# An elementwise sum moved from VectorE to an accumulating DMA, with its consumers a quarter-step later

## The chip, the cores and the metric

The kernel runs on one core of a Trainium2 chip. The metric is device time of one execution in microseconds, where less is better: the median of three runs before the change is 296.59 us (296.36 to 297.35).

## What is computed

Attention over 4 batches, 8 heads, 768 positions and head size 64, in which each query sees the first 4 positions and a window of its own last 128, is followed by a two-layer block on the 3072 x 512 result. The part that the change touches is the function between the two matrix products, a quotient of polynomials taken for every one of 3072 x 2048 elements:

```
h = x @ w_in                      # 3072 x 512 by 512 x 2048
P = a[0] + a[1]*h + a[2]*h*h + a[3]*h*h*h
Q = 1 + |b[0]|*|h| + |b[1]|*h*h
g = P / (Q + 1e-6)
out = g @ w_out                   # 3072 x 2048 by 2048 x 512
```

## The kernel before, in words

The 3072 rows are cut into NSTEP = 12 steps of 256 rows. For each step there is an attention part (scores, exponentials, a mask, the product with v, a normalization, a transpose) and a part of the block: the first GEMM (`project_in`, L419), the function, and the second GEMM (`project_out`, L500). h of a step is one tile `hb` of 128 partitions x 4096 columns in bf16, and all intermediate tiles of the function (`sq`, `den`, `num`, `g`) have this shape. One such tile is 1 MB.

The order on every engine is written out by hand in one loop over t, a "slot". Four slots make a step: t = 4p + j. In slot t, TensorE computes a quarter of the first GEMM of step p, some scores and attention products of steps ahead, and a quarter of the second GEMM of an older step; ScalarE copies h out of PSUM, takes exponentials, and takes the reciprocal of Q as exp(-ln Q) in two passes; VectorE does the polynomials. With c = p - 1, the function runs through these places:

- j = 0: `magnitude` (L449) and `square` (L443) of half B of step c, `recip_den` (ScalarE, L486) of half B of step c - 1, `denominator` (L454) of half A
- j = 1: `log_den` (ScalarE, L480) of half A, `denominator` of half B, and `gate(c - 1)` (L492), g = num * (1/Q)
- j = 2: `log_den` of half B, `even(c)` (L460), which writes num = a2*h² + a0, and `odd(c)` (L465), which turns sq into a3*h² + a1
- j = 3: `odd_h(c)` (L470), sq = sq*h, then `numerator(c)` (L474), num = num + sq, and the first half of the next square on ScalarE (L441)

Between these VectorE also normalizes the attention results as they come (L381, L384), multiplies masks (L348) and spreads transposed k (L293). Each engine takes its instructions in the written order, so an instruction that waits holds up all that stand behind it. `num` has a single buffer: even(c) can't write before gate(c - 1) has read.

`project_out` of step m starts in slot 4m + 10, the slot after gate(m), as `back = t - 10` says, and takes four slots, two for each 128 rows. `store` copies a finished result from PSUM (ScalarE, L505) and sends it off (L507).

DMAs are issued from two places. SP's queue carries the stores and the transposes of x (L407), k (L284) and q (L265). GpSimd's queue (POOL) carries the loads that cast from float32 to bf16: w_in, w_out, k (L131), q (L118) and v (L151). In slot 4p + 2, `feed` puts two loads of k and two of q on it, six steps ahead of c; in slot 4p, `load_v` puts eight loads of v on it. A load waits until its buffer is free: k and q for the transposes that read the buffer before, v for the attention products of an older step.

The numbers of the loop that the change touches:

```
for t in range(NSLOT + 14):
    back = t - 10
```

Of the kernel before, what the change touches and what calls it, by code (L numbers as in the profile page):

```python
# [13 lines left out]
ALU = mybir.AluOpType  # L14
# [3 lines left out]
def kernel(  # L18
# [13 lines left out]
    nc = tc.nc  # L32
# [130 lines left out]
    def load_w_out(part):  # L163
        for c in range(part * NFFC // 2, (part + 1) * NFFC // 2):
            nc.gpsimd.dma_start(out=w_out_sb[c], in_=moe_w_out[c * P:(c + 1) * P, :])
# [20 lines left out]
    for e in range(2):  # L186
        lo = e * 64
        nc.gpsimd.affine_select(
            out=edge[lo:lo + 64, 0, :], in_=edge[lo:lo + 64, 0, :], pattern=[[1, 64]],
            compare_op=ALU.is_ge, fill=0.0, base=0, channel_multiplier=-1)  # L190
        nc.gpsimd.affine_select(
            out=edge[lo:lo + 64, 1, :], in_=edge[lo:lo + 64, 1, :], pattern=[[-1, 64]],
# [12 lines left out]
    for h in range(H):  # L205
        nc.gpsimd.dma_start(out=v_sink[16 * h:16 * h + NS, :, h, 0:D],
                            in_=v[:, h, 0:NS, :].rearrange("b s d -> s b d"))
# [78 lines left out]
    def spread_k(s):  # L286

        b, g = divmod(s, GPB)
        src = kT_flat.pop(s)
        kT = kT_fix[s % 2]  # L290
        for e in range(2):
            lo, hi = e * 64, (e + 1) * 64
            nc.vector.tensor_copy(out=kT[lo:hi, :, lo:hi],  # L293
                                  in_=src[lo:hi].rearrange("p i (j c) -> p (i j) c", c=64))
        if g == 0:
            nc.vector.tensor_copy(
                out=k_sink[b % 2].rearrange("p (i c) -> p i c", c=160)[:, :, 0:32].rearrange(
                    "p i (e s) -> p i e s", e=2)[:, :, :, 0:NS],
                in_=kT.rearrange("p (i n) (e s) -> p i n e s", n=NHF, e=2)[:, :, 0, :, 0:NS])
# [112 lines left out]
    hb, sq, den, num, g_of, lnq, ps_h, ps_out = {}, {}, {}, {}, {}, {}, {}, {}  # L412

    def project_in(m, j):
        ps = ps_hp.tile([P, GC, TS], FP32, tag="ps_h", name="ps_h")
        for n in range(GC):
            fc = j * GC + n
            for c in range(NDMC):
                nc.tensor.matmul(ps[:, n, :], lhsT=w_in_sb[c][:, fc * P:(fc + 1) * P],  # L419
                                 rhs=xblk[m][:, c, :], start=(c == 0), stop=(c == NDMC - 1))  # L420
        ps_h[m, j] = ps
# [7 lines left out]
    def cols(w, part=None):  # L429

        if part is None:
            return slice(0, MW)
        k_, n = part
        return slice(k_ * MW // n, (k_ + 1) * MW // n)

    def square(m, part, eng):
        if m not in sq:
            sq[m] = m_sb.tile([P, MW], BF16, tag="sq", name="sq")
        c = cols(MW, part)
        if eng == "act":  # L440
            nc.scalar.activation(out=sq[m][:, c], in_=hb[m][:, c], func=AF.Square)  # L441
        else:
            nc.vector.tensor_tensor(out=sq[m][:, c], in0=hb[m][:, c], in1=hb[m][:, c], op=ALU.mult)  # L443

    def magnitude(m, part=None):
        if m not in den:
            den[m] = m_sb.tile([P, MW], BF16, tag="den", name="den")
        c = cols(MW, part)
        nc.vector.tensor_scalar(out=den[m][:, c].bitcast(U32), in0=hb[m][:, c].bitcast(U32),  # L449
                                scalar1=0x7FFF7FFF, scalar2=None, op0=ALU.bitwise_and)  # L450

    def denominator(m, part=None):
        c = cols(MW, part)
        nc.vector.tensor_tensor(out=den[m][:, c], in0=den[m][:, c], in1=sq[m][:, c], op=ALU.add)  # L454
# [16 lines left out]

    def numerator(m, part=None):
        c = cols(MW, part)
        nc.vector.tensor_tensor(out=num[m][:, c], in0=num[m][:, c], in1=sq[m][:, c], op=ALU.add)  # L474

    def log_den(m, part):
        c = cols(MW, part)
        t_ = m_sb.tile([P, HW], FP32, tag="lnq", name="lnq")
        lnq[m, part] = t_[:, 0:c.stop - c.start]
        nc.scalar.activation(out=lnq[m, part], in_=den[m][:, c], func=AF.Ln, scale=qsc,  # L480
                             bias=one_eps)

    def recip_den(m, part):
        c = cols(MW, part)
        with nc.allow_low_precision(reason="exp(-ln(q)) reciprocal, tol 2e-2"):
            nc.scalar.activation(out=den[m][:, c], in_=lnq[m, part], func=AF.Exp, scale=-1.0)  # L486
# [16 lines left out]
    def store(m, tt):  # L503
        o_t = o_sb.tile([P, DM], FP32, tag="o_t", name="o_t")
        nc.scalar.activation(out=o_t, in_=ps_out.pop((m, tt)), func=AF.Copy)  # L505
        row0 = m * TS + tt * P
        nc.sync.dma_start(out=out[row0:row0 + P, :], in_=o_t)  # L507
# [6 lines left out]
    NSLOT = 4 * NSTEP  # L514
# [3 lines left out]
    def feed(s):  # L518
        if s < NSTEP:
            load_k(s)  # L520
            for n in (2 * s + 1, 2 * s + 2):
                if n < NQT:
                    load_q(n)

    def turn_qk(s):
        if s < NSTEP:
            turn_k(s)
            for n in (2 * s + 1, 2 * s + 2):
                if n < NQT:
                    turn_q(n)  # L530
# [13 lines left out]
    def do_mask(n):  # L544
        s, i = divmod(n, NPB)
        if s < NSTEP and i % 2 == 1:
            mask(s, i // 2)
# [6 lines left out]
    def do_norm(n):  # L554
        s, i = divmod(n, NPB)
        if s < NSTEP:
            normalize(s, i)
            if i % 2 == 1:
                turn_x(s, i // 2)
# [48 lines left out]
    turn_at = {0: 2, 2: 3, 4: 4, 6: 5}  # L608
    stored = []
    prev_s, prev_a = (), ()  # L610
    for t in range(NSLOT + 14):
        p, j = divmod(t, 4)
        in_m = p < NSTEP
        ns = ahead_s.get(t, (t + 8,))
        na = ahead_a.get(t, (t + 6,))
        c = p - 1
        in_c = 0 <= c < NSTEP
        in_g = 0 <= c - 1 < NSTEP
        back = t - 10
        in_o = 0 <= back < NSLOT  # L620
        if stored:
            store(*stored.pop(0))
        for n in prev_a:
            do_norm(n)
        for n in prev_s:
            do_mask(n)
        if in_m:
            project_in(p, j)
        late = t > 7 and (t + 10) % NPB == 0
        if t == 0:  # L630
            turn_qk(1)
            spread_k(1)
        s = spread_at.get(t, (t + 10) // NPB if late else NSTEP)
        if s < NSTEP:
            spread_k(s)
        s = turn_at.get(t, (t + 14) // NPB if late else NSTEP)
        if s < NSTEP:
            turn_qk(s)
            if s != 3:
                feed(s + 2)  # L640
        if t in (4, 5):
            load_w_out(t - 4)
        if t == 5:
            feed(5)

        if j == 0:
            if in_c:
                magnitude(c, B_)
                square(c, B_, "dve")
            if in_g:  # L650
                recip_den(c - 1, B_)
            if in_c:
                denominator(c, A_)
        if j == 1:
            if in_c:
                log_den(c, A_)
                denominator(c, B_)
            if in_g:
                gate(c - 1)
        if j == 2:  # L660
            if in_c:
                log_den(c, B_)
                even(c)
        if j == 3:
            if in_c:
                recip_den(c, A_)
        if in_m:
            copy_in(p, j)
        if t < 4:
            for n in ns:  # L670
                do_sinks(n)
                do_scores(n)
                do_mask(n)
            for n in na:
                do_attend(n)
                if n != na[-1]:
                    do_norm(n)
        else:
            for n in ns:
                do_sinks(n)  # L680
                do_scores(n)
        if j == 2 and in_m:
            magnitude(p, A_)
        if in_o:
            m, gq = divmod(back, 4)
            tt, part = divmod(gq, 2)
            project_out(m, tt, part * NFFC // 2, (part + 1) * NFFC // 2)
            if part == 1:
                stored.append((m, tt))
        if t >= 4:  # L690
            for n in na:
                do_attend(n)
                if n != na[-1]:
                    do_norm(n)
        if j == 2 and in_c:
            odd(c)
        if j == 3:
            if in_c:
                odd_h(c)
                numerator(c)  # L700
            if in_m:
                square(p, A_, "act")
        prev_s = ns if t >= 4 else ()
        prev_a = na[-1:]
        if t >= 3 and (t == 3 or t > 4 and t % NPB == 0):
            s = 3 if t == 3 else (t + 8) // NPB
            if 3 <= s < NSTEP:
                load_v(s)
# [33 lines left out]
```

The softmax here doesn't subtract the row's maximum and nothing guards it: scores larger than these inputs give would overflow.

## Time and profile before

| | |
|---|---|
| median of three runs | 296.59 us |
| profiled execution, its own time | 298.49 us |
| its span | 296.8 us |
| mean granted TensorE clock | 0.96 |
| `numerator` L474 | 12 instructions, 27.5 us, 2292 ns each |
| `gate` L492 | 12 instructions, 27.4 us, 2284 ns each |
| loads of v, k, q from POOL | 4.4, 5.4 and 5.9 us from issue to landing (medians) |
| stores, 256 KB each | 2.4 us to landing (median) |
| chain that ended last, by engine | DVE 56%, PE 16%, DMA 8%, ACT 7%, issue 6%, SPq 5% |

In the profile, PE is TensorE, DVE VectorE, ACT ScalarE and POOL GpSimd; SPq is SP's queue. "L474" is line 474 of the kernel. A timeline line has the start and the length in microseconds, the engine, the line, the operation, what it writes and reads, and in brackets the idle time before it with what ended it. In a table of stretches each engine's busy time is given in microseconds, with the number of instructions. The ends of matmuls are modelled, so PE's busy time is an upper bound on its work.

### The profile page before, as it was taken

The numbers are of one execution on the slowest core, as the hardware profiler recorded it, in microseconds if no ns is written. First come the engines' busy times: TensorE is split into PE (matmuls) and PEld (weight loads), VectorE is DVE, ScalarE is ACT, GpSimd is POOL, SyncE is SP. The second block draws the span as 40 slices with busy tenths as digits, with TensorE's granted clock in tenths as the row PEclk, the third lists the DMA queues.
The fourth block names the chain that finished last, engine by engine and source line by source line (L and its number), as shares of the span: only waits on it lengthen the run. The fifth ranks groups of instructions, "written<-read, shape, count | busy, mean of one in ns | idle before, by whom it ended". The sixth has DMA issues, their size and how long they took to land.

```text
span 296.8 us, 4876 instructions
## 1 busy us (share of the span) xinstructions
PE 235.5 (79%) x1856; PEld 167.4 (56%) x1876; DVE 239.3 (81%) x320; ACT 214.2 (72%) x201; POOL 116.1 (39%) x178
## 2 busy tenths in 40 slices
PE   0516866658609899999989899998999999997864
PEld 0414555546507777767767677676677767652321
DVE  6606623736794999999999999999999999999930
ACT  2104261684735998989979899898998989897810
POOL 8938668879091046181651793380000000000000
PEclk9999997996957999999999999999999999997999
DMA  8999999999999199398995999292110121100111
GB/s 160 127 171 80 157 127 158 142 171 201 143 114 47 29 129 128 80 136 108 116 103 105 147 107 121 27 140 63 55 41 17 53 55 53 38 35 35 71 38 72
DMA packets 116632, 28.94 MB, mean 98 GB/s; under 512 B 110464, under 2 KB 112512, under 8 KB 116608
## 3 DMA queue, kind: packets, MB, share of 16 engines
q0 software_dynamic: 72752, 12.74, 64.1%
q1 hardware_dynamic: 43856, 15.88, 26.6%
q8 instruction: 15, 0.25, 0.4%
q14 instruction: 9, 0.07, 0.1%
HBM read 27.30 MB, written 6.29 MB: 113 GB/s over the span
## 4 chain that ended last, share of the span: by engine, by line
DVE 56%; PE 16%; DMA 8%; ACT 7%; issue 6%; SPq 5%; POOL 1%; DVEq 0%; ACTq 0%; POOLq 0%
DVE sq L470 8%; DVE num L474 8%; PE ps_h L419 7%; DVE g L492 6%; DVE den L454 6%; DVE x_n L384 5%; DVE num L460 4%; DVE den L449 4%; DVE e L348 4%; PE ps_out L500 4%; DVE sq L443 3%; PE ps_o L371 3%; DMA b_bc<-in_moe_b_dram 3%; DVE sq L465 2%; ACT hb L426 2%
## 5 line engine op out<-in xcount | busy, mean ns | idle before, releaser
L419 PE MATMUL ps_h<-xblk,w_in_sb 128*128 128x256 bf16 x768 | 98.5, 284 | 8.3 <-DMA xblk<-x_n 7.5
L500 PE MATMUL ps_out<-w_out_sb,g 128*128 128x512 bf16 x364 | 87.8, 385 | 7.6 <-ACT o_t L505 4.0
L419 PEld LDWEIGHTS <-w_in_sb 128*128 128x128 bf16 x768 | 76.4, 102 | 20.5 <-DMA xblk<-x_n 7.8
L151 POOL DMA_DIRECT2D v_bd<-in_v_dram x88 | 57.3, 670 | 28.7 <-PE ps_o L371 12.2
L426 ACT ACTIVATE hb<-ps_h 128x1024 bf16<-128x1024 f32 x48 | 49.1, 1022 | 26.2 <-PE ps_h L419 26.2
L500 PEld LDWEIGHTS <-g 128*128 128x128 bf16 x384 | 37.3, 99 | 45.6 <-issue 7.0
L480 ACT ACTIVATE lnq<-den,one_eps,qsc 128x2048 f32<-128x2048 bf16 x24 | 50.4, 2098 | 10.9 <-DVE den L454 10.9
L486 ACT ACTIVATE den<-lnq 128x2048 bf16<-128x2048 f32 x24 | 46.2, 1924 | 0.0
L341 ACT ACTIVATE e<-ps_s 128x768 bf16<-128x768 f32 x48 | 38.9, 816 | 2.8 <-PE ps_s L331 2.8
L131 POOL DMA_DIRECT2D k_bf<-in_k_dram x22 | 20.3, 937 | 46.9 <-DMA kT_flat<-k_bf 46.6
L371 PE MATMUL ps_o<-v_bd,e 128*128 128x130 bf16 x352 | 31.4, 228 | 9.1 <-DVE x_n L384 4.2
L331 PE MATMUL ps_s<-qT,kT 128*128 128x192 bf16 x192 | 25.7, 260 | 14.9 <-ACT e L341 14.6
L371 PEld LDWEIGHTS <-e 128*128 128x128 bf16 x352 | 26.1, 102 | 19.4 <-DVE x_n L384 4.9
L454 DVE TENSOR_TENSOR den<-den,sq 128x2048 bf16<-128x2048 bf16 x24 | 29.0, 1215 | 0.0
L331 PEld LDWEIGHTS <-kT 128*128 128x128 bf16 x192 | 18.4, 104 | 17.7 <-issue 16.2
L474 DVE TENSOR_TENSOR num<-num,sq 128x4096 bf16<-128x4096 bf16 x12 | 27.5, 2292 | 0.4
L492 DVE TENSOR_TENSOR g<-num,den 128x4096 bf16<-128x4096 bf16 x12 | 27.4, 2284 | 0.1
L470 DVE TENSOR_TENSOR sq<-sq,hb 128x4096 bf16<-128x4096 bf16 x12 | 27.4, 2284 | 0.1
L384 DVE SCALAR_TENSOR_TENSOR x_n<-ps_o,csc,rec 128x256 bf16<-128x256 f32 x48 | 23.2, 484 | 1.7
L381 DVE RECIPROCAL rec<-ps_o 128x4 f32<-128x4 f32 x48 | 8.5, 177 | 18.7 <-PE ps_o L371 18.5
L348 DVE TENSOR_TENSOR e<-e,edge 128x1024 bf16<-128x1024 bf16 x24 | 16.4, 683 | 8.3 <-ACT e L341 8.3
L441 ACT ACTIVATE sq<-hb 128x2048 bf16<-128x2048 bf16 x12 | 22.9, 1910 | 0.0
(67 smaller groups left out, 205.8 us busy)
## 6 DMA issues: line engine op xcount, KB each, us to landing
out_dram<-o_t SPq DMA_DIRECT2D x24, 256.0 KB, 2.4
k_bf<-in_k_dram POOLq DMA_DIRECT2D x22, 128.0 KB, 5.4
v_bd<-in_v_dram POOLq DMA_DIRECT2D x88, 32.0 KB, 4.4
q_bf<-in_q_dram POOLq DMA_DIRECT2D x21, 128.0 KB, 5.9
w_in_sb<-in_moe_w_in_dram POOLq DMA_DIRECT2D x8, 256.0 KB, 7.6
w_out_sb<-in_moe_w_out_dram POOLq DMA_DIRECT2D x16, 128.0 KB, 5.0
stage_q<-in_q_dram SPq DMA_DIRECT2D x3, 256.0 KB, 5.2
xblk<-x_n SPq DMA_TRANSPOSE x40, 3.5
```

The costliest lines, as they stand in the source:

```text
L151: nc.gpsimd.dma_start(out=t_[lo:hi, i, :, e, 0:D], in_=src)
L331: nc.tensor.matmul(ps[:, n // 2, (n % 2) * 192:(n % 2) * 192 + 192], lhsT=kT_fix[s % 2][:, i * NHF + n, :], rhs=qT_fix[b % 2][:, i, c:c + ...
L371: nc.tensor.matmul(ps_o[:, n, :], lhsT=l_, rhs=r_.rearrange("p e c -> p (e c)"), start=(m == 0), stop=(m == len(terms) - 1))
L419: nc.tensor.matmul(ps[:, n, :], lhsT=w_in_sb[c][:, fc * P:(fc + 1) * P], rhs=xblk[m][:, c, :], start=(c == 0), stop=(c == NDMC - 1))
L426: nc.scalar.activation(out=hb[m][:, j * GW:(j + 1) * GW], in_=ps_h.pop((m, j)).rearrange("p n c -> p (n c)"), func=AF.Copy)
L454: nc.vector.tensor_tensor(out=den[m][:, c], in0=den[m][:, c], in1=sq[m][:, c], op=ALU.add)
L470: nc.vector.tensor_tensor(out=sq[m][:, c], in0=sq[m][:, c], in1=hb[m][:, c], op=ALU.mult)
L474: nc.vector.tensor_tensor(out=num[m][:, c], in0=num[m][:, c], in1=sq[m][:, c], op=ALU.add)
L480: nc.scalar.activation(out=lnq[m, part], in_=den[m][:, c], func=AF.Ln, scale=qsc, bias=one_eps)
L486: nc.scalar.activation(out=den[m][:, c], in_=lnq[m, part], func=AF.Exp, scale=-1.0)
L492: nc.vector.tensor_tensor(out=g_of[m][:, c], in0=num[m][:, c], in1=den[m][:, c], op=ALU.mult)
L500: nc.tensor.matmul(ps_out[m, tt], lhsT=g_of[m][:, co:co + P], rhs=w_out_sb[fc], start=(fc == 0), stop=(fc == NFFC - 1))
```

## The change

`numerator` no longer runs on VectorE. It becomes a DMA from GpSimd's queue that reads `sq` and adds it into `num`, both in SBUF. The row of 4096 bf16 elements is cut at 4096 bytes, so that the compiled DMA is 128 x 2 x 2048 elements. There are twelve of them, one for each step, and in GpSimd's written order the one of step c stands behind the k and q loads of slot 4p + 2 and before the eight v loads of slot 4(p + 1).

`gate(c - 1)` moves from slot j = 1 to slot j = 2, where it stands before even(c) and behind that slot's normalization, mask and spread. `project_out` and with it the stores move one slot later, and the loop has one slot more.

```
     def numerator(m, part=None):
         c = cols(MW, part)
-        nc.vector.tensor_tensor(out=num[m][:, c], in0=num[m][:, c], in1=sq[m][:, c], op=ALU.add)
+        nc.gpsimd.dma_start(out=num[m][:, c], in_=sq[m][:, c], accum_op=ALU.add, max_dma_last_dim=4096)
...
-    for t in range(NSLOT + 14):
+    for t in range(NSLOT + 15):
...
-        back = t - 10
+        back = t - 11
...
             if in_c:
                 log_den(c, A_)
                 denominator(c, B_)
+        if j == 2:
             if in_g:
                 gate(c - 1)
-        if j == 2:
             if in_c:
                 log_den(c, B_)
                 even(c)
```

More of the change, by code (lines that the diff above doesn't have):

```diff
@@ L473, in numerator @@
         c = cols(MW, part)
-        nc.vector.tensor_tensor(out=num[m][:, c], in0=num[m][:, c], in1=sq[m][:, c], op=ALU.add)
+        nc.gpsimd.dma_start(out=num[m][:, c], in_=sq[m][:, c], accum_op=ALU.add, max_dma_last_dim=4096)
     def log_den(m, part):
@@ L610 @@
     prev_s, prev_a = (), ()
-    for t in range(NSLOT + 14):
+    for t in range(NSLOT + 15):
         p, j = divmod(t, 4)
@@ L618 @@
         in_g = 0 <= c - 1 < NSTEP
-        back = t - 10
+        back = t - 11
         in_o = 0 <= back < NSLOT
@@ L657 @@
                 denominator(c, B_)
+        if j == 2:
             if in_g:
                 gate(c - 1)
-        if j == 2:
             if in_c:
```

## The prediction

> **What bounds the kernel now.** I read first the busy times of the engines.
>
> ```profile
> PE 235.5 (79%) x1856; PEld 167.4 (56%) x1876; DVE 239.3 (81%) x320; ACT 214.2 (72%) x201; POOL 116.1 (39%) x178
> ```
>
> No engine stands out over the whole span, so I went to stretches: one step in mid-run, and the last two between numerators.
>
> ```profile
> core 0: us, PE busy (x) PEld busy (x) DVE busy (x) ACT busy (x) POOL busy (x), PEclk, DMA share, GB/s
> 199.80:218.30 18.50, 17.48 (x146) 12.60 (x146) 18.27 (x23) 17.10 (x17) 0.00 (x0) 1.00 0.23 53
> 252.50:266.60 14.10, 13.97 (x95) 9.20 (x95) 13.99 (x11) 13.26 (x11) 0.00 (x0) 1.00 0.10 38
> 266.60:280.20 13.60, 9.68 (x36) 3.87 (x36) 13.46 (x9) 12.10 (x10) 0.00 (x0) 0.87 0.10 39
> ```
>
> In mid-run VectorE is full (18.27 of 18.50 us) and sets the pace; but TensorE is close behind (17.48) and so is ScalarE (17.10). The removed add is 2.29 us a step, but TensorE gives back at most about 1 us of it. In the stretch from 252.5 TensorE is as full as VectorE (13.97 of 14.10): nothing is to be had. The same table for all steps gives period and TensorE's floor: 18.8/18.3, 18.5/17.8, 18.7/17.4, 19.2/18.4 (steps 1 to 4, from 106 to 181 us), 18.6/17.9, 18.5/17.5, 17.8/17.3 (5 to 7), 16.4/16.3 (8).
>
> Next, VectorE's timeline for the loop that the change closes.
>
> ```profile
> 207.83 2.28 DVE L492 TENSOR_TENSOR g<-num,den 128x4096 bf16<-128x4096 bf16 x1
> ...
> 212.22 1.35 DVE L460 TENSOR_SCALAR num<-sq,acoef 128x4096 bf16<-128x4096 bf16 x1
> ...
> 215.95 2.28 DVE L470 TENSOR_TENSOR sq<-sq,hb 128x4096 bf16<-128x4096 bf16 x1
> 218.26 2.29 DVE L474 TENSOR_TENSOR num<-num,sq 128x4096 bf16<-128x4096 bf16 x1
> ...
> 226.29 2.29 DVE L492 TENSOR_TENSOR g<-num,den 128x4096 bf16<-128x4096 bf16 x1
> ```
>
> From the end of the sum (220.5) to gate are 5.8 us of other work; from gate's end (210.1) to even (212.2) 2.1 us, which in the new order stand before gate. Last, the tail:
>
> ```profile
> 280.20 2.29 DVE L474 TENSOR_TENSOR num<-num,sq 128x4096 bf16<-128x4096 bf16 x1
> 282.62 2.29 DVE L492 TENSOR_TENSOR g<-num,den 128x4096 bf16<-128x4096 bf16 x1
> ...
> 284.97 3.63 PE L500 MATMUL ps_out<-w_out_sb,g 128*128 128x512 bf16 x16 [1.92 <-DVE g L492]
> ```
>
> Here sum, gate and second GEMM follow one another with nothing between them. In the chain of work that ended last, the pieces before are the same VectorE ladder.
>
> **What the new DMA costs.** Call L the time from the end of odd_h (L470) to the moment when gate may start. The trace has no accumulating DMA and none within SBUF of this size. Its parts: the smallest recent load from this queue gives issue, descriptors and completion:
>
> ```profile
> v_bd<-in_v_dram POOLq DMA_DIRECT2D x4, 32.0 KB, 3.0
> ```
>
> (DMA issues from 196 to 215 us, where the queues are nearly empty: 3.0 us from issue to landing.) The Trainium skill, "DMA: Bandwidth & Descriptors", section "Anatomy of one DMA — SWDGE (gpsimd) path", fits 2.0 us plus bytes at 436 GB/s; the fixed part is less than this trace's 3.0, and I take 3.0. The skill's "Collectives: The Full Stack", section "The bandwidth ceiling: the fold count and why AG ≠ RS ≠ AR", says that an add in the DMA engine needs two source reads for each write and so halves the rate; no run here shows it. Two times 1.05 MB at 436 GB/s is an estimate of 4.8 us. With 0.5 us for sharing the engines with transposes and stores, L = 3.0 + 4.8 + 0.5 = **8.3 us**. Bounds: 5.9 us if the add runs like a plain copy (2.4 us of data and the rest), and about 13 if the adder takes twice the estimate (9.6 us of data). "DMA: Bandwidth & Descriptors", section "SDMA does more than copy", gives no rate for the adder, only a limit of 2048 elements, the size of the pieces here, so nothing excludes the slow end.
>
> **Part by part.**
>
> *Removed:* 12 sums, 12 x 2.29 = 27.5 us of VectorE. VectorE's step falls to about 16.2 us, under TensorE's floor.
>
> *Added, a loop with latency:* num has one buffer and VectorE runs in order, so gate(c-1), even(c), odd(c), odd_h(c), the DMA and gate(c) form a closed chain. Gate, 2.3 us, plus 212.22 to 218.23, 6.0 us, makes 8.3 us in mid-run: the period can't be under 8.3 + L = 16.6 us. That is below the floor of 17.3 to 18.4, so mid-run the DMA is covered by TensorE's work; the cover ends at L = 9.6 or so. What waits behind a late gate: even, odd, odd_h and the next normalization, for which TensorE's attention waits in turn.
>
> *Steps 5 to 7:* to the floor: -0.7 - 1.0 - 0.5 = **-2.2 us**.
>
> *Steps 1 to 4:* GpSimd's queue is in the way. Its timeline at step 2:
>
> ```profile
> 125.03 1.78 POOL L131 DMA_DIRECT2D k_bf<-in_k_dram  x2 [8.72 <-DMA kT_flat<-k_bf]
> 126.91 0.88 POOL L118 DMA_DIRECT2D q_bf<-in_q_dram  x1
> 128.69 0.87 POOL L118 DMA_DIRECT2D q_bf<-in_q_dram  x1 [0.90 <-DMA qT<-q_bf]
> 129.55 3.71 POOL L151 DMA_DIRECT2D v_bd<-in_v_dram  x6
> ```
>
> The k loads wait for transposes of their own slot, and the new DMA stands behind them: it could be issued at 129.55, while odd_h ended at 124.75. Part of these 4.8 us goes when odd_h itself comes later, since the transposes don't wait for gate. The loads' data lie ahead of it in the same queue (q takes 5.2 us to land here against 3.0 of an idle queue), so I add 0 to 4 us to L: periods of 16.6 (then the floor) to 20.6, against 18.8 on average. From -3.3 to +7.6 us over four steps; the middle of the added delay, 2 us, gives 18.6, and I take **0**.
>
> *Steps 8 to 10, where attention runs out:* the same chain without normalizations. Step 8: 7.75 + 8.3 = 16.05, floor 16.3, before 16.4: 0. Step 9: gate at 258.77 to odd_h's end at 266.54 is 7.8; 7.8 + 8.3 = 16.1 against 14.1: **+2.0**. Step 10: gate at 272.79 to 280.15 is 7.4; 15.7 against 13.6: **+2.1**. The cover is gone here, because the work between sum and gate is only 4.0 us (254.77 to 258.77).
>
> *The end:* odd_h ends at 280.15 and gate starts at 282.62, 2.5 us; with the DMA 8.3: **+5.8 us**.
>
> *Moved:* gate and project_out a slot later add no instructions. Twelve gates keep their place between odd_h and even; g has two buffers, so its late readers cost nothing. The extra slot holds nothing else: its 32 matmuls follow the last gate as before. Stores move by a slot on SP, where each takes 0.33 us of issue; SP's queue waits 86.6 us for results between 100 and 280 us, so nothing is late.
>
> *Step 0:* gate(0) at 95.2 moves to about 100, and even(1) from 100.0 to 102.3; the removed sum gives it back by 108.3. 0. The v loads behind the first DMA can be late by 1 to 3 us; that is a rival below.
>
> *The SBUF port:* the skill's "SBUF — State Buffer", section "SBUF: two separate sides", warns that VectorE's fast modes can hold up GpSimd's descriptor writing. The v loads keep 0.61 us each beside a full VectorE, so I add nothing.
>
> Sum: -2.2 + 0 + 2.0 + 2.1 + 5.8 = +7.7 us. Against the profiled execution, 298.49 + 7.7 = 306.2; its time is 1.9 above the median, so the same difference gives **304.3 us**.
>
> **Rivals.**
>
> *The adder is slow (B).* L of 13: mid-run periods 21.3 (4 steps +2.5 and three +3.0, together +19), step 8 +4.4, then +6.7 and +6.8, the end +10.5: about +47, 344 us. For it: no row prices the adder, and the loop multiplies each microsecond by up to ten. Against: the skill's halving accounts for the reads alone. It begins at L = 9.6 and grows by 10 us for each us.
>
> *The DMA is quick, and it is faster (C).* One place decides: L from odd_h to gate. With L = 5.9, steps 1 to 4 reach the floor (-3.3), 5 to 7 -2.2, steps 8 to 10 -0.5, the end +3.4: -2.6, 294.0 us. It turns at L near 6.5. For it: DMA share is 0.10 to 0.23 in the late stretches. Against: even 32 KB took 3.0 us, and 1 MB has to be read twice.
>
> *Loads are pushed back (D).* Eight v loads stand behind each sum, on one queue and the same rings, and from 106 to 181 us the DMA engines are full (DMA share 0.99 to 1.51). TensorE would wait for v: five steps by 2 us on top of +7.7, 314 us. For it: the loads for step 4 are issued up to 91 us, land some 5 us later, and are read at about 101. Against: v has over a slot of slack later, where the queue waits for TensorE and not the reverse.
>
> **How the numbers follow.** Likeliest case 0.45 (L 7 to 9.6, 298 to 311 us), B 0.33, C 0.12, D 0.10. The range to which all but 2 in 10 belong: down to 295, cutting off most of C, and up to 345, cutting off the half of B beyond L = 13. What a measurement of this kernel tells from no change is about 0.3%. Slower: 0.45 + 0.33 + 0.10 less 0.04 for the lower edge near 6.5, so 0.84; same 0.04; faster 0.12.
>
> **What would show it.** Twelve L474 DMAs from POOL, landing 7 to 8 us after issue. VectorE without L474, and with idle time before gate, L492, released by this DMA: near none in steps 5 to 8, 2 us in steps 9 and 10, 5.8 at the end. Mid-run periods between gates 17.3 to 18.4 with TensorE over 95% busy. Wrong if landings take over 10 us, if gate waits in every step, or if TensorE waits for v.

## The result

The changed kernel takes 323.5 us (median of four runs, 321.38 to 324.04) against 296.48 us before: a ratio of 1.089, with a 95% interval of 1.084 to 1.095. The prediction was 304.3 us, in a range of 295 to 345. The direction was right; of a change of +27 us it foresaw +7.7. Runs that came out over 1.5% longer than the fastest of their kernel are left out of all medians and ratios.

The profile after, from its page: the busy times, the queue that carries the new DMA, the chain that ended last, the two lines that the change touched, and two kinds of DMA with their time to landing.

```profile
PE 244.1 (76%) x1876; PEld 169.0 (52%) x1876; DVE 212.4 (66%) x308; ACT 215.6 (67%) x201; POOL 130.3 (40%) x190
...
q0 software_dynamic: 76016, 25.33, 83.1%
...
DMA 34%; DVE 21%; PE 21%; ACT 9%; SPq 7%; issue 5%; POOL 1%; DVEq 0%; POOLq 0%; ACTq 0%
...
L474 POOL DMA_DIRECT2D num<-sq x12 | 15.7, 1312 | 80.3 <-DVE rec L381 32.1
L492 DVE TENSOR_TENSOR g<-num,den 128x4096 bf16<-128x4096 bf16 x12 | 27.5, 2293 | 28.3 <-DMA num<-sq 28.2
...
num<-sq POOLq DMA_DIRECT2D x12, 1024.0 KB, 9.8
...
v_bd<-in_v_dram POOLq DMA_DIRECT2D x88, 32.0 KB, 9.4
```

VectorE did get its 27 us back (239.3 to 212.4 us), and no engine is busier than 76%. The chain that was 56% VectorE is now 34% DMA. The new DMA takes 9.8 us to land, gate waits 28.2 us for it, and the v loads take 9.4 us where they took 4.4.

The table of stretches of the changed kernel, for the same places as before (a mid-run step, the last two between two sums, and the tail):

```profile
core 0: us, PE busy (x) PEld busy (x) DVE busy (x) ACT busy (x) POOL busy (x), PEclk, DMA share, GB/s
...
207.90:226.50 18.60, 17.86 (x151) 12.68 (x149) 16.11 (x23) 17.33 (x17) 6.36 (x9) 1.00 1.15 114
...
262.90:280.60 17.70, 14.63 (x84) 8.33 (x82) 11.77 (x10) 14.99 (x13) 1.21 (x1) 0.90 0.42 90
280.60:296.60 16.00, 8.63 (x31) 3.37 (x31) 11.29 (x9) 8.55 (x6) 1.20 (x1) 0.79 0.46 98
296.60:322.20 25.60, 13.56 (x51) 5.18 (x49) 2.31 (x2) 2.39 (x4) 1.19 (x1) 0.87 0.35 83
```

In mid-run VectorE is relieved (18.27 to 16.11 us), yet the step takes 18.6 us, not less than the 18.5 of before. VectorE's timeline of the late steps shows the closed chain, with gate waiting for the DMA:

```profile
278.33 2.29 DVE L470 TENSOR_TENSOR sq<-sq,hb 128x4096 bf16<-128x4096 bf16 x1
289.24 2.29 DVE L492 TENSOR_TENSOR g<-num,den 128x4096 bf16<-128x4096 bf16 x1 [4.60 <-DMA num<-sq]
291.57 1.35 DVE L460 TENSOR_SCALAR num<-sq,acoef 128x4096 bf16<-128x4096 bf16 x1
294.33 2.29 DVE L470 TENSOR_TENSOR sq<-sq,hb 128x4096 bf16<-128x4096 bf16 x1
305.73 2.29 DVE L492 TENSOR_TENSOR g<-num,den 128x4096 bf16<-128x4096 bf16 x1 [9.11 <-DMA num<-sq]
```

From the end of odd_h to gate, L of the prediction, are 289.24 - 280.62 = 8.6 us and 305.73 - 296.62 = 9.1 us here. In the early steps gate waits too:

```profile
121.18 2.29 DVE L492 TENSOR_TENSOR g<-num,den 128x4096 bf16<-128x4096 bf16 x1 [2.71 <-DMA num<-sq]
140.66 2.29 DVE L492 TENSOR_TENSOR g<-num,den 128x4096 bf16<-128x4096 bf16 x1 [0.95 <-DMA num<-sq]
161.32 2.29 DVE L492 TENSOR_TENSOR g<-num,den 128x4096 bf16<-128x4096 bf16 x1 [2.21 <-DMA num<-sq]
180.72 2.29 DVE L492 TENSOR_TENSOR g<-num,den 128x4096 bf16<-128x4096 bf16 x1 [0.53 <-DMA num<-sq]
```

L is 13.2, 11.1, 12.3 and 11.1 us in these four steps. In mid-run it is 10.2 us (207.93 to 218.15), but there gate comes when VectorE has finished its other work, and waits for nothing. A second thing shows in TensorE's timeline of the tail:

```profile
308.08 5.82 PE L500 MATMUL ps_out<-w_out_sb,g 128*128 128x512 bf16 x16 [6.66 <-DVE g L492]
314.63 3.61 PE L500 MATMUL ps_out<-w_out_sb,g 128*128 128x512 bf16 x16 [0.73 <-ACT o_t L505]
```

The first 16 matmuls of the last second GEMM take 5.82 us after 6.66 us of idle time, the other 16 take 3.61 us after 0.73 us.

Where the time went, by the ends of odd_h in the two timelines, and in the run `no_sum` below, which has the new schedule and no sum at all (us, from the profiled executions; changes are taken before rounding):

| from odd_h of step ... to | before | after | no_sum | predicted change | measured change |
|---|---|---|---|---|---|
| 0 to 1 | 23.0 | 25.0 | 21.8 | 0 | +2.0 |
| 1 to 5 | 75.2 | 81.1 | 74.9 | 0 | +5.9 |
| 5 to 8 | 54.8 | 56.1 | 54.9 | -2.2 | +1.2 |
| 8 to 9 | 16.4 | 17.8 | 15.7 | 0 | +1.4 |
| 9 to 10 | 14.1 | 17.7 | 11.8 | +2.0 | +3.6 |
| 10 to 11 | 13.6 | 16.0 | 12.0 | +2.1 | +2.4 |
| odd_h(11) to gate(11) | 2.5 | 9.1 | 0.7 | +5.8 | +6.6 |
| gate(11) to the end | 14.2 | 16.5 | 16.9 | 0 | +2.3 |
| sum | | | | +7.7 | +25.4 |

The sum of the last column is the difference of the spans, 322.2 - 296.8. The late steps, 9 to 11, came near what was forecast for them. What failed is everything that was booked at nothing or as a gain: steps 0 to 8 and the tail. (The 16.9 us at the end of no_sum have another reason than the 16.5 of the changed kernel: there gate(11) comes so early that TensorE still has older second GEMMs to finish, at 3.61 us for 16 matmuls.)

### The profile page after: what moved, and what is told of

The parts are those of the page before. It is cut to its first block, busy times and chain, and to the rows that moved or that the text cites. A ratio compares the mean times of both kernels' runs of the same rounds, so it can differ in the third digit from the quotient of the medians.

```text
span 322.2 us, 4924 instructions
## 1 busy us (share of the span) xinstructions
PE 244.1 (76%) x1876; PEld 169.0 (52%) x1876; DVE 212.4 (66%) x308; ACT 215.6 (67%) x201; POOL 130.3 (40%) x190
## 4 chain that ended last, share of the span: by engine, by line
DMA 34%; DVE 21%; PE 21%; ACT 9%; SPq 7%; issue 5%; POOL 1%; DVEq 0%; POOLq 0%; ACTq 0%
DMA num<-sq 21%; PE ps_h L419 8%; PE ps_out L500 7%; DVE g L492 5%; DVE sq L470 5%; PE ps_o L371 4%; DMA v_bd<-in_v_dram 4%; DMA out_dram<-o_t 3%; DMA b_bc<-in_moe_b_dram 3%; SPq L407 3%; DVE sq L465 3%; ACT hb L426 2%; DVE x_n L384 2%; ACT e L341 2%; DVE num L460 2%
## 5 line engine op out<-in xcount | busy, mean ns | idle before, releaser
L500 PE MATMUL ps_out<-w_out_sb,g 128*128 128x512 bf16 x384 | 95.5, 397 | 18.5 <-DVE g L492 16.4
L151 POOL DMA_DIRECT2D v_bd<-in_v_dram x88 | 59.6, 1012 | 52.2 <-DMA num<-sq 38.5
L500 PEld LDWEIGHTS <-g 128*128 128x128 bf16 x384 | 38.2, 101 | 60.9 <-DVE g L492 17.7
L474 POOL DMA_DIRECT2D num<-sq x12 | 15.7, 1312 | 80.3 <-DVE rec L381 32.1
L371 PE MATMUL ps_o<-v_bd,e 128*128 128x130 bf16 x352 | 32.8, 234 | 19.6 <-DMA v_bd<-in_v_dram 8.0
L492 DVE TENSOR_TENSOR g<-num,den 128x4096 bf16<-128x4096 bf16 x12 | 27.5, 2293 | 28.3 <-DMA num<-sq 28.2
L505 ACT ACTIVATE o_t<-ps_out 128x512 f32<-128x512 f32 x24 | 14.4, 600 | 30.1 <-PE ps_out L500 30.0
L131 POOL DMA_DIRECT2D k_bf<-in_k_dram x22 | 20.6, 946 | 31.8 <-DMA kT_flat<-k_bf 30.7
L331 PEld LDWEIGHTS <-kT 128*128 128x128 bf16 x192 | 18.1, 103 | 17.2 <-issue 15.9
L384 DVE SCALAR_TENSOR_TENSOR x_n<-ps_o,csc,rec 128x256 bf16<-128x256 f32 x48 | 23.2, 484 | 1.7
```

Source lines behind the costliest of these rows:

```text
L151: nc.gpsimd.dma_start(out=t_[lo:hi, i, :, e, 0:D], in_=src)
L331: nc.tensor.matmul(ps[:, n // 2, (n % 2) * 192:(n % 2) * 192 + 192], lhsT=kT_fix[s % 2][:, i * NHF + n, :], rhs=qT_fix[b % 2][:, i, c:c + ...
L371: nc.tensor.matmul(ps_o[:, n, :], lhsT=l_, rhs=r_.rearrange("p e c -> p (e c)"), start=(m == 0), stop=(m == len(terms) - 1))
L384: nc.vector.scalar_tensor_tensor(out=dst, in0=o4[:, :, 0:D].rearrange("p (n e) c -> p n e c", e=2), scalar=csc, in1=rec.rearrange("p (n e) ...
L492: nc.vector.tensor_tensor(out=g_of[m][:, c], in0=num[m][:, c], in1=den[m][:, c], op=ALU.mult)
L500: nc.tensor.matmul(ps_out[m, tt], lhsT=g_of[m][:, co:co + P], rhs=w_out_sb[fc], start=(fc == 0), stop=(fc == NFFC - 1))
```

## The experiments

Ratios are against the kernel before on the same chip, with 95% intervals. Three theories stood against each other. Latency: the wait for the DMA in the closed chain. Traffic: loads and transposes delayed by the DMA. The move: gate and project_out a slot later cost time by themselves.

**The move alone, and no sum at all.** Edits to the changed kernel: the sum back on VectorE, and the sum left out.

```
     def numerator(m, part=None):
-        nc.gpsimd.dma_start(out=num[m][:, c], in_=sq[m][:, c], accum_op=ALU.add, ...)
+        nc.vector.tensor_tensor(out=num[m][:, c], in0=num[m][:, c], in1=sq[m][:, c], op=ALU.add)   # move_only
+        pass                                                                                       # no_sum
```

> Only the move: the sum stays on VectorE, gate and project_out stand a slot later. The latency theory (most of the 27 us is the wait for the DMA in the closed chain) and the traffic theory (most of it is loads and transposes delayed by the DMA) both expect 296 to 298 us, at most 0.5% from the kernel before. The move theory expects 300 us or more: the last gate stands a slot, some 4 us, later.

> The schedule of the changed kernel without any sum, so the output leaves out the odd part of the numerator. It bounds what taking the sum off VectorE can bring. If TensorE's floor of 17.3 to 18.4 us a step holds, as the prediction said, 288 to 292 us; if VectorE's relief were fully usable, 296 - 27 = 269 us or a little more.

Measured: move_only 317.8 us, ratio 1.065 (1.060 to 1.071). no_sum 297.4 us, 0.997 (0.995 to 1.000). Move_only went the way of the move theory, but far beyond the 300 us that it had named, and no_sum lies above both of its expectations: with the sum on VectorE the move by itself costs 19 us, and with VectorE 27 us lighter the new schedule only draws level with the old. The step of move_only is 21.0 us in mid-run against 18.5. Its VectorE timeline shows where the 2.5 us lie:

```profile
200.24 1.22 DVE L454 TENSOR_TENSOR den<-den,sq 128x2048 bf16<-128x2048 bf16 x1
202.95 0.16 DVE L320 TENSOR_TENSOR e_sink<-e_sink,sink_edge 128x4 bf16<-128x4 bf16 x1 [1.49 <-ACT e_sink L318]
203.73 0.18 DVE L381 RECIPROCAL rec<-ps_o 128x4 f32<-128x4 f32 x1 [0.62 <-PE ps_o L371]
...
205.82 2.29 DVE L492 TENSOR_TENSOR g<-num,den 128x4096 bf16<-128x4096 bf16 x1
208.15 1.49 DVE L460 TENSOR_SCALAR num<-sq,acoef 128x4096 bf16<-128x4096 bf16 x1
209.55 0.72 DVE L449 TENSOR_SCALAR den<-hb 128x1024 uint32<-128x1024 uint32 x1
210.19 1.33 DVE L465 TENSOR_SCALAR sq<-sq,acoef 128x4096 bf16<-128x4096 bf16 x1
```

In slot j = 1 VectorE has only half a denominator left, and then waits for TensorE and ScalarE (1.49 + 0.62 us). In slot j = 2, from 203.73 to the next normalization at 211.44, it has 7.7 us of work, in which TensorE's next attention products, which need the normalization to free their one PSUM buffer, can't go on. In the groups of instructions, VectorE's waits for attention products (ps_o) rise from 18.5 us before to 34.9 us, and ScalarE's for the denominator from 10.9 to 30.0 us.

No_sum also prices the DMA, since the changed kernel differs from it in the DMA alone: 27.5 us between the profiled executions. Gate's waits for the DMA are 28.2 us together. They fit step by step: less its four waits of 6.4 us the changed kernel would take 74.7 us from odd_h(1) to odd_h(5), and no_sum takes 74.9. So in this schedule the DMA costs what gate waits for it, in the early steps as in the late ones. TensorE's waits for v, 8.0 us in 7 places of the changed kernel, add almost nothing to that.

**The unwaited sum, with its control.** From the kernel before: even(c) writes g's tile, gate multiplies in place, the freed num tile takes the twelve DMAs (side_sum), or nothing is summed (side_none).

```
-        nc.vector.tensor_tensor(out=num[m][:, c], in0=num[m][:, c], in1=sq[m][:, c], op=ALU.add)
+        nc.gpsimd.dma_start(out=side[0][:, c], in_=sq[m][:, c], accum_op=ALU.add, max_dma_last_dim=4096)   # side_sum
+        pass                                                                                             # side_none
```

> Control for the next: schedule of the kernel before, even(c) writes the tile of g and gate multiplies in place, no sum at all (the output leaves out the odd part of the numerator). Both theories expect about what the schedule of before gives without the sum, 287 to 292 us.

> As the control, with the twelve accumulating DMAs of 1 MB from sq into a tile that nobody reads (the output leaves out the odd part of the numerator): all the traffic and GpSimd's queue as in the changed kernel, but gate waits for no DMA. Latency theory: within 4 us of the control, since only loads and transposes are slower. Traffic theory: 15 us or more above the control, with TensorE waiting for v and for x.

Measured: side_none 287.3 us, 0.963 (0.958 to 0.968); side_sum 307.4 us, 1.034 (1.026 to 1.041). The control confirms the prediction's TensorE floor: its steps 1 to 7 take 17.1 to 18.1 us. So taking the sum off VectorE is worth 3.7%, some 11 us, in the old schedule, if it costs nothing elsewhere. The DMAs cost some 20 us although gate doesn't wait for them, and they cost it between the odd_h of steps 1 and 6 (19.9, 23.2, 21.3, 24.4, 20.7 us against 18.0, 17.7, 17.2, 18.1, 17.6); from step 6 on the two runs agree within 0.4 us a step. The table of waits of side_sum (us in total, times, the longest) names TensorE waiting for v:

```profile
PE ps_o L371 <- DMA v_bd<-in_v_dram: 16.1, 4, 5.8
```

In the control there is no such line. This is the prediction's rival D, at about twice its size, but in a schedule in which gate doesn't wait. In the changed kernel gate's wait comes first and hides it, by the account above.

**The v loads ahead of the sum.** The same edit, which also issues the loads two slots earlier, was made to the changed kernel (v_early) and to the unwaited sum (side_sum_v):

```
+        if t >= 10 and t % NPB == 2 and (t + 10) // NPB < NSTEP:
+            load_v((t + 10) // NPB)
         s = turn_at.get(t, (t + 14) // NPB if late else NSTEP)
...
-        if t >= 3 and (t == 3 or t > 4 and t % NPB == 0):
-            s = 3 if t == 3 else (t + 8) // NPB
-            if 3 <= s < NSTEP:
-                load_v(s)
+        if t in (3, 8):
+            load_v(3 if t == 3 else 4)
```

> The changed kernel with the v loads from step 5 on written two slots earlier, ahead of the k and q loads and of the accumulating DMA in GpSimd's queue instead of behind it. Theory traffic: the v loads wait for the DMA's completion and for its data, and TensorE waits for v (8.0 us in 7 waits); it expects 4 to 8 us less than the changed kernel, 315 to 320 us, and waits for v under 2 us. Theory latency: no more than 2 us, since gate's wait stays.

> The run with the unwaited accumulating DMAs (308.9 us; its control without them 287.3 us; both leave out the odd part of the numerator), with the v loads from step 5 on written ahead of the k and q loads and of the DMA. If the loss is TensorE waiting for v behind the sum: 289 to 295 us and no waits for v. If it is the DMA engines shared with loads and transposes: 302 us or more.

Measured: v_early 323.4 us, 1.086 (1.075 to 1.097), no gain; side_sum_v 295.0 us, 0.989 (0.985 to 0.993), some 12 us less than side_sum. In both, no wait for v is left. That the changed kernel gains nothing agrees with the account above: its waits for v were not what held it up. Gate's waits for the DMA are 27.1 us in v_early too; one sum lands 5.1 us late for its gate, and that step takes 24.2 us. In side_sum_v 7.7 us over the control remain, and the table of waits has something else for them:

```profile
PE ps_h L420 <- DMA xblk<-x_n: 15.7, 5, 7.1
```

TensorE now waits for the transposed x, which landed in 5.9 us in place of the control's 3.7 (medians), in five places against one (7.0 us, early in the run) in the control. So more than half of what the traffic costs in the old schedule was the place of v in GpSimd's queue; for the rest the transposes that share the DMA engines with the sum are the likely cause, but no run took them away. In the queue of the changed kernel the order is plain:

```profile
109.66 0.88 POOL L118 DMA_DIRECT2D q_bf<-in_q_dram  x1 [1.07 <-DVE e L348]
110.53 1.26 POOL L474 DMA_DIRECT2D num<-sq  x1
111.25 4.90 POOL L151 DMA_DIRECT2D v_bd<-in_v_dram  x7
121.44 0.62 POOL L151 DMA_DIRECT2D v_bd<-in_v_dram  x1 [5.29 <-DMA num<-sq]
```

odd_h(1) ended at 107.98, and the sum was issued at 110.53, behind k and q, 2.6 us later; in steps 2 to 4 it was 0.6 to 1.2 us. From issue to gate are 10.5 to 11.1 us in these four steps, against 8.1 to 9.3 in the last four. The eighth v load waits until the sum has landed, in every step that has v loads (38.5 us in 8 waits).

**The late steps back on VectorE.** `numerator` takes the DMA for m < 8 only.

> The changed kernel with the sums of the last four steps (8 to 11) back on VectorE. Theory latency: where attention runs out nothing covers the DMA; in the changed kernel steps 8 to 10, the last wait for gate and the last GEMM cost 16 us against the kernel before, so 306 to 309 us. If the late part is instead the price of the move, 318 us or more.

Measured: 310.0 us, 1.038 (1.028 to 1.048); against the changed kernel's 1.089 that is some 5% or 15 us. This confirms the latency theory for the late part: steps 9 and 10 are back at 14.1 and 13.6 us, and gate(11) follows as before. The rest of the loss stays.

**The adder's price.** The same DMA without `accum_op`, a plain copy over num.

> The changed kernel with a plain copy of sq to num of the same shape in place of the accumulating DMA (the even part of the numerator is lost). It prices the adder: if the second read is what takes time, a 4 KB piece takes about half of the 350 ns that it takes in the changed kernel, landing falls by 2.5 to 3 us to about 7, and the run takes 308 to 314 us. If the fixed parts make up the landing time, nothing changes: landing 9 to 10 us, 322 us.

Measured, with two executions only: 306.6 us, 1.030 (1.022 to 1.037), and landing in the list of DMA issues:

```profile
num<-sq POOLq DMA_DIRECT2D x12, 1024.0 KB, 6.4
```

Adding costs 3.4 us a landing and 17 us a run; gate's waits fall from 28.2 to 11.1 us. In the trace's packet records, a 4 KB piece takes 353 ns when it is added and 161 ns when it is copied (medians of 3072): a factor of 2.2, near the halving that the Trainium skill gives in "Collectives: The Full Stack", section "The bandwidth ceiling: the fold count and why AG ≠ RS ≠ AR". Of the 9.8 us, 16 pieces an engine at 353 ns are 5.6 us, against the 4.8 us estimated; the other 4 us, which were not taken apart, had been put at 3.5.

**What in the move costs.** The kernel before with project_out and the stores alone a slot later (late_gemm); the move with even(c) brought to j = 1, where gate had been (move_balanced; num then lies in a third buffer of g); and the same with odd(c) brought to j = 1 too (even_dve):

```
 # late_gemm: back = t - 11, gate stays in j == 1
 # move_balanced, even_dve: gate in j == 2, back = t - 11, and
         if j == 1:
             if in_c:
                 log_den(c, A_)
                 denominator(c, B_)
+                even(c)
+                odd(c)        # even_dve only
```

In even_dve the last two gates, behind which no first GEMM runs, stand in j = 1 ahead of even.

> The kernel before with only project_out and its stores a slot later; gate stays in slot j = 1 and the sum on VectorE. Theory 1 (the move costs because gate's 2.3 us went into VectorE's fullest slot): 296 to 299 us. Theory 2 (TensorE's own order costs): 305 us or more, towards the 317.8 of the whole move.

> The move alone again (sum on VectorE, gate and project_out a slot later, which cost 19 us), but with even(c) taken from slot j = 2 to j = 1, where gate stood. For this, num lies in a third buffer of g, since the one buffer of num would force even behind gate. Theory 1, uneven slots: the move put 7.5 us of VectorE work into slot j = 2 and left 1.7 us in j = 1, while TensorE and VectorE hand over slot by slot; it expects the 19 us to vanish, 296 to 300 us. Theory 2, TensorE's order: project_out, its PSUM copies and stores stand a slot later; it expects 312 us or more still.

> Gate in slot j = 2 and project_out a slot later, as in the changed kernel, all sums on VectorE, but even and odd in slot j = 1 (num in a third buffer of g): VectorE's work by slot is about 4.1, 4.4, 4.9 and 5.1 us. If uneven slots were the whole price of the move, 295 to 299 us; if gate in j = 2 costs by itself, 303 us or more.

Measured: late_gemm 297.8 us, 1.000 (0.997 to 1.003); move_balanced 307.4 us, 1.033 (1.028 to 1.039); even_dve 299.7 us, 1.007 (1.005 to 1.010). TensorE's new order costs nothing. Partly evened slots give back half of the move's price (6.5% to 3.3%), fully evened ones nearly all of it (0.7%). So the price was not gate's late place in itself, which even_dve keeps, but that slot j = 2 was overfull and j = 1 nearly empty. The third buffer, without which even could not be written ahead of gate, was not tried alone. The 2 us of even_dve over the kernel before are not explained.

**The cold TensorE.** In the changed kernel, 30 matmuls on weights, into a buffer that nobody reads, ahead of the last second GEMM.

```
+            if m == NSTEP - 1 and tt == 0:
+                ps_w = ps_mp.tile([P, DM], FP32, tag="ps_m", name="ps_warm")
+                for n in range(30):
+                    nc.tensor.matmul(ps_w, lhsT=w_out_sb[n % NFFC][:, 0:P], rhs=w_out_sb[n % NFFC], start=True, stop=True)
```

> The changed kernel with 30 matmuls of 128x512 on weights, into a PSUM bank that nobody reads, written ahead of the last step's second GEMM, to keep TensorE at work while it waits for the last gate (it was idle for 6.7 us there). In the changed kernel the first 16 matmuls after that idle time took 5.8 us, in the kernel before, after 1.9 us of idle time, 3.6 us. If idleness is the cause, these 16 take 3.6 to 3.8 us again and the run 321 us, 2 us less; if not, they stay at 5.8 us and the run at 323 us.

Measured: 325.2 us, 1.090 (1.085 to 1.094), so no gain in the total. The local effect is there, in TensorE's timeline:

```profile
302.69 6.64 PE L501 MATMUL ps_warm<-w_out_sb 128*128 128x512 bf16 x30
311.37 3.63 PE L505 MATMUL ps_out<-w_out_sb,g 128*128 128x512 bf16 x15 [2.04 <-DVE g L492]
```

After 2.04 us of idle time the first half of the GEMM takes 3.63 us, and from gate(11) to the end are 14.3 us in place of 16.5. Idleness is the cause of the tail's last 2.2 us. The total doesn't show it: in this execution the early steps were slower (odd_h(5) ended at 191.3 us against 189.1), and the last gate waited 11.1 us for its DMA in place of 9.1. Whether the added matmuls lengthened that landing was not tested. The Trainium skill, "TensorE: Matmul & The Clock Gate", section "Part 1: The HAM clock gate (the "warmup" mystery)", has the rule: after about 3.4 us without work TensorE's clock falls to half, and matmuls of 512 columns then follow each other at 426.7 ns. The changed kernel's trace agrees on the halved clock and the spacing: behind the 6.66 us gap the granted clock is 0.50 (308.1 to 311.9 us), then 1.00, and weight loads follow each other at 0.42 to 0.43 us (308.48, 308.91, 309.33). On the length of the gap the traces say more than the 3.4 us: gaps of 1.9 and 2.0 us cost nothing, but in the changed kernel a gap of 2.83 us (ended at 275.11) already left the next 16 matmuls at a granted clock of 0.50 and 5.24 us, while 2.98 us in even_dve left them at 3.61; at 2.38 us they took 5.30 in even_mix and 3.61 in no_sum. What decides between 2.4 and 3 us is not shown.

**Both causes taken away.** First, open_all and open_mix: even(c) in j = 1, gate(c - 1) in j = 3 behind odd_h(c), project_out two slots later, so that a DMA has a whole step to land; steps 0 to 9 or 6 to 9 by DMA, most of the others on VectorE in j = 1 of the next step.

```
         if j == 1:
             if in_c: log_den(c, A_); denominator(c, B_)
             ...
+            if in_c: even(c)
         ...
         if j == 3:
             if in_c: odd_h(c); numerator(c)
+            if in_g and p < NSTEP: gate(c - 1)
+            if in_m: magnitude(p, A_)
```

> The chain opened and the slots evened: num lies in a third buffer of g, even(c) stands in slot j = 1, gate(c - 1) in j = 3 behind odd_h(c) and the DMA's issue, so that a DMA has a whole step to land; project_out two slots later. Steps 0 to 9 by DMA, 10 and 11 on VectorE. Theory latency plus uneven slots: nothing is left of the loss, 288 to 294 us. Theory traffic: steps 1 to 5, in which loads of v, k and q go through the same queue, stay at 20 to 24 us a step as in the run with the unwaited sum, so 303 to 310 us.

> As the run before, but only steps 6 to 9 by DMA, where no loads of k and q are left; steps 0 to 5, 10 and 11 on VectorE (the sum of step c in slot j = 1 of the next step). The unwaited sum cost nothing in steps 6 to 11. If that holds for a sum that is used, steps 6 to 9 take 17.2, 17.1, 15.7 and 13.3 us in place of 18.4, 17.8, 16.4 and 14.1 of the kernel before, and the run 292 to 295 us, under the kernel before. If the new order of VectorE costs as the move did, 300 us or more.

Measured: open_all 308.7 us, 1.033 (1.027 to 1.039): with no gate held up, steps 1 to 4 still take 20.2 to 22.4 us, the traffic again, now in the open, with 9.5 us of TensorE's waits for v. open_mix 298.1 us, 1.000 (0.998 to 1.003): no gain. Its steps 6 and 7 take 18.5 and 18.7 us, with VectorE waiting 4.8 us for attention products in place of 0.2 before. Gate and magnitude made j = 3 heavy; that this is the cause was not tested.

Then the evened order of even_dve with a DMA for steps 5 to 8 (even_mix), and for steps 1 to 8 with the v loads ahead (even_all_v):

```
     def numerator(m, part=None):
+        if m in by_dma:        # (5, 6, 7, 8), or (1, ..., 8)
+            nc.gpsimd.dma_start(out=num[m][:, c], in_=sq[m][:, c], accum_op=ALU.add, max_dma_last_dim=4096)
+        else:
+            nc.vector.tensor_tensor(...)
```

> The evened kernel with the sums of steps 5 to 8 by DMA, where few or no loads are in the queue, the others on VectorE. Chain of gate, odd_h, DMA and gate: 5.8 + 10 = 15.8 us, under the step. If both causes are understood, these four steps fall by 0.7 to 1.2 us each and the run is 292 to 294 us, under the kernel before. If the DMA costs there too, 297 us or more.

> The same with steps 1 to 8 by DMA and the v loads ahead. If v behind the sum was the loss of the early steps, they gain 1 us each as well: 288 to 292 us. If the shared DMA engines are the cause, 298 us or more.

Measured: even_mix **295.4 us, 0.991 (0.987 to 0.994)**, 0.9% under the kernel before and clear of the noise; even_all_v 302.0 us, 1.013 (1.008 to 1.017). The stretch from odd_h(5) to odd_h(9) of even_mix, and then of even_dve, with the columns of the table of stretches above:

```profile
180.50:248.30 67.80, 67.80 (x578) 49.84 (x576) 62.67 (x78) 65.07 (x59) 20.16 (x28) 1.00 1.07 135
```

```profile
181.70:253.60 71.90, 69.38 (x580) 49.80 (x578) 70.83 (x82) 65.66 (x60) 8.93 (x14) 1.00 0.39 64
```

With the sum on VectorE the four steps take 71.9 us and VectorE is busy for 70.8; by DMA they take 67.8 us and TensorE is busy throughout. In these steps this is all that the change can gain: the floor is TensorE's. In even_all_v the early steps wait again, for the sum itself:

```profile
DVE g L494 <- DMA g<-sq: 14.8, 4, 4.5
```

Its four waits lie in steps 1 to 4, whose sums were issued 2.3 to 5.0 us after odd_h, behind the k and q loads. For the early steps no order was found that gains.

## Why the prediction was wrong

Three prices, taken apart in this order, make up the change: the sum off VectorE in the old schedule, -11 us (side_none); the move without a sum, +10 us (no_sum against side_none); the DMA in the new schedule, some +27 us, nearly all of it gate's wait. The prediction had -2 for the first, nothing for the second and +10 for the third. Against its +7.7 us the profiled executions differ by +25.4, and the 17.7 us between lie as follows.

- **"L = 8.3 us", the term that was mis-sized: some 10 us.** The closed chain was the right mechanism. But L was 13.2, 11.1, 12.3 and 11.1 us in steps 1 to 4, where the prediction had put 0 to 4 us on top of 8.3 and taken the middle. The chain gives 8.3 + 11.9 = 20.2 us a step on average; 20.3 were measured, and 18.8 booked ("Steps 1 to 4: 0", measured +5.9). Of this L, 0.6 to 2.6 us passed before the issue, behind the k and q loads, and 10.5 to 11.1 us were the landing, for which 7 to 8 had been expected. In the late steps L was 9.9, 9.9, 8.6 and 9.1 us: step 8 measured +1.4 for 0, and what was +9.9 from step 9 to gate(11) measured +12.6. Too small were the data (5.6 us for 4.8) and the fixed part with the other transfers (some 4 us for 3.5).
- **"Moved: gate and project_out a slot later add no instructions", the step that failed outright.** It counted instructions and asked what gate's readers need, but not how much VectorE already had in slot j = 2. The profile of before had it: 5.2 us of work in j = 2 without gate, about 4 in j = 1 with it. With the sum on VectorE the move costs 6.5%, 19 us, without it 10 us, which is all of the relief but 1 us. So in this schedule even a DMA that nobody waits for could have brought 0.3% at most. Steps 5 to 7 came out at +1.2 us rather than -2.2: no_sum, in which there is nothing to wait for, takes 54.9 us there against 54.8 before, and gate's waits for the DMA in these steps (0.3, none and 0.8 us) are the other 1.1.
- **The sum's removal, right.** The floor that TensorE sets was right: without any sum and in the old schedule (side_none) steps 5 to 7 took 17.6, 17.2 and 17.1 us; 17.9, 17.5 and 17.3 had been read from the busy times.
- **"Step 0: 0", failed by 2.0 us.** odd_h(1) ended at 108.0 us against 106.0, and in no_sum at 107.8. In the eight profiled executions with the move and its uneven slots it ended at 107.3 to 109.0 us, in the ten others at 104.5 to 106.5: this belongs to the move too.
- **"Its 32 matmuls follow the last gate as before", failed by 2.3 us.** They follow, but at half the clock at first, since the longer wait for gate let TensorE cool down. A wait that grows from 1.9 to 6.7 us costs more than its length.
- **Nothing on SP, right** in the sense that no store was late; but the x transposes on SP's queue landed in 5.8 us in place of 3.5.
- **The rivals.** D, loads pushed back, is real wherever gate does not wait (side_sum, open_all); in the changed kernel it is hidden behind gate's wait. B, a slow adder, had L at 13 in every step; this was reached in one. C, a gain, was to turn at L near 6.5, which left the move out: with no sum at all the new schedule is level with the old kernel. Of the signs of being wrong that were named, TensorE did wait for v, gate waited in ten steps of twelve, and some landings took over 10 us.
- **Slips without weight.** Four periods of 20.6 us are 7.2 us above the 75.2 of before, not 7.6; gate(9) starts at 258.69, not 258.77.

## What to carry to other kernels

Before an instruction is moved to make room for a latency, add up what its engine already does in the slot where it goes: where two engines hand over slot by slot through one buffer, an uneven slot costs its excess in every step. Where a DMA stands in a closed chain, price its landing beside the transfers that will run with it, and expect to pay all by which it outlasts the work between; a second delay can lie hidden behind that wait and come out when the wait is taken away. Move only the steps in which nothing stands ahead of the DMA in its queue and other work outlasts the landing. Relief of the fullest engine is worth no more than the distance to the next one, here 4 us over four mid-run steps.

## What the runs showed of the hardware that was not expected

- A 1 MB accumulating DMA within SBUF lands 9.8 us after issue (median; 8.0 to 11.1), a plain copy of the same shape in 6.4 us (median). A 4 KB piece takes 353 ns added and 161 ns copied.
- 16 matmuls of 128x512 take 5.8 us after 6.7 us of TensorE idle time, and 3.6 us after 2.0 us or less; after 2.8 us they took 5.2 us. The prediction had not counted the clock.
- Between the end of odd_h and the issue of the DMA that waits for it lie 0.54 to 0.57 us even when GpSimd's queue was idle (207.93 to 208.49, 296.62 to 297.16), in six steps of seven; in the other, step 9, 1.08 us.
